# Early scores, a second queue for the moves, and a last product in halves

## The chip, the cores and the metric

One core of a Trainium2 chip runs the whole program. The metric is device time in microseconds. Five engines matter: TensorE (matmuls, in rows of the profile PE, its weight loads PEld), VectorE (DVE), ScalarE (ACT), GpSimd (POOL, nearly unused here) and SyncE (SP), which issues most transfers; a transfer can also be issued by ScalarE, and such rows have the engine name ACTq.

## The reference

`x` is 8 batches x 8 heads x 512 tokens x 64, `state` 8 x 8 x 32 x 64. For each batch and head:

```
a     = softmax(x state^T / 8)  over the 32 states;   xread = a state        (512 x 64)
a2    = softmax(state x^T / 8)  over the 512 tokens;  sread = a2 x           (32 x 64)
rows  = concat(xread, sread), heads side by side: 8 x 544 rows of 512
h     = rows w_in          (512 x 2048)
out   = (h * clip(h + 3, 0, 6) / 6) w_out     (2048 x 512)
```

All in float32, 4352 rows out.

## The kernel before

**Tiling.** `rows w_in` is not formed from `xread`: for the tokens, `state w_in` (called W', `wprime`) is made first and the softmax weights `aT` are multiplied with it. The work is a list of `steps`, each one batch and one block of 128 columns of `w_in`: `first(n)` makes h for 512 tokens in one of two `ps_h` banks, ScalarE and VectorE turn it into g (lines 908 and 910) and split g into two float32r halves (lines 246 and 247), and `second(n)` multiplies them with `w_out` into four accumulators `acc0` to `acc3`, two steps later (`LAG`). Each float32 product is three float32r matmuls (`product`, line 858). The chunk of 4 steps for batch 0 alone, steps 0 to 3, uses plain float32 (lines 887 and 927), because the halves of its weights are not ready then. The steps run: batch 0 chunk 0, batch 1 chunks 0 and 1, batch 0 chunks 1 to 3, batch 1 chunks 2 and 3, then batches 2 to 7, and last the `sread` rows of all batches (b equal to B, 256 rows, 2 accumulators).

**Scores.** For each batch the scores x state^T are wanted twice. `scores_by_columns` puts them with states along the partitions, 16 matmuls into two banks (`all_heads`, line 462); `states(b)` makes the softmax over tokens from them: maximum (714), exponential (718), sums and reciprocals (721, 723). `tokens_by_rows` (batch 0, line 620) and `tokens_by_columns` (batch 1 and later) make the softmax over states, lines 574 to 591, and turn it into `aT` (639 and 644 for batch 0). For batch 1 the scores by columns are copied out of PSUM (line 686) and kept for `states(1)`; for batch 0 they are made a second time, inside `late`, told at step 8 with rank 2.35 and name "L", in the two `ps_s` banks, and `states(0)` reads them there. Line 540 (`put_state`) copies a batch's turned state out of PSUM; line 555 turns x and line 560 copies it.

**Moves.** `weights_moved(1)` turns the exponentials of batch 1 block by block: VectorE transposes 32 x 32 blocks (766), then 32 small transfers of 16 KB (line 773), all issued by SP, place the blocks; `tokens_read(1)` (line 815) reads the result, in one go on TensorE with batch 2's scores.

**Order.** Nothing is scheduled by hand and nothing by the hardware: `Plan` collects operations with an engine (T, V, S, Q for TensorE, VectorE, ScalarE, SP), a cost in us, a rank and the tiles they read and write. `order` then goes through a model of the time: for each engine it takes, among the operations that can start within 0.3 us of the earliest (0.8 for ranks up to 0), the one with the lowest rank; `URGENT` is rank -20. Slots of tiles are limited: `st_raw` has one, `tmp` ten, each accumulator one. What comes out is a fixed order of instructions on every engine; an instruction that has to wait holds up all behind it on its engine. Until the first product TensorE is kept at work with transposes of the identity into a spare bank (line 1157, `idle`). The rank of a step's work is its number n; the weights' ranks stand in the table `weights` (told, kind, block, blocks, place, rank of preparing, rank of loading), prepared on ScalarE and VectorE by lines 308 to 327 and split by 352 and 354.

**The end.** For b equal to B the two accumulators are evicted by VectorE (`acc0`, line 954) and ScalarE (`acc1`, line 951), scaled by 1/6, and stored by SP and by ScalarE (both rows show line 969).

## Time and profile before

| | us |
|---|---|
| median of 3 runs (659.68 to 659.81) | 659.69 |
| the profiled execution | 660.08 |
| its span, first to last instruction | 658.2 |
| TensorE busy (98%) | 647.7 |
| VectorE busy (64%) | 420.4 |
| ScalarE busy (47%) | 312.1 |

The granted TensorE clock is 0.999 of full speed, that is 2.4 GHz throughout. Matmuls are pipelined and their ends modelled: a matmul of 512 columns has a row of 0.39 us, but the next one starts 0.23 us later, so starts are to be compared, not durations. `PE ps_h L887 x4` is four matmuls of line 887 that write a `ps_h` bank. In a timeline row the brackets give the idle time just before the instruction and who ended it. A line can be that of a helper.

### The profile page before, as it was taken

The numbers are of one execution on the slowest core, as the hardware profiler recorded it, in microseconds if no ns is written. First come the engines' busy times: TensorE is split into PE (matmuls) and PEld (weight loads), VectorE is DVE, ScalarE is ACT, GpSimd is POOL, SyncE is SP. The second block draws the span as 40 slices with busy tenths as digits, with TensorE's granted clock in tenths as the row PEclk, the third lists the DMA queues.
The fourth block names the chain that finished last, engine by engine and source line by source line (L and its number), as shares of the span: only waits on it lengthen the run. The fifth ranks groups of instructions, "written<-read, shape, count | busy, mean of one in ns | idle before, by whom it ended". The sixth has DMA issues, their size and how long they took to land.

```text
span 658.2 us, 9905 instructions
## 1 busy us (share of the span) xinstructions
PE 647.7 (98%) x3934; PEld 502.1 (76%) x3934; DVE 420.4 (64%) x697; ACT 312.1 (47%) x522; POOL 1.0 (0%) x7
## 2 busy tenths in 40 slices
PE   7999999999999999999999999999999999999997
PEld 7447777777777877787877877787778788788896
DVE  4999999977756845954577356934595353443552
ACT  5889686643524543533444343534344343333542
POOL 0000000000000000000000000000000000000000
PEclk9999999999999999999999999999999999999999
DMA  8904742415163043323050504041131001000101
GB/s 266 318 1 160 196 150 106 98 27 138 19 144 58 15 75 85 66 32 65 17 116 14 83 1 121 13 64 32 64 66 28 5 1 65 0 1 1 64 1 33
DMA packets 130895, 46.26 MB, mean 70 GB/s; under 512 B 119201, under 2 KB 121249, under 8 KB 130721
## 3 DMA queue, kind: packets, MB, share of 16 engines
q1 hardware_dynamic: 130704, 45.37, 27.9%
q8 instruction: 31, 0.51, 0.3%
q10 hardware_dynamic: 144, 0.26, 0.1%
q14 instruction: 16, 0.12, 0.1%
HBM read 33.03 MB, written 8.91 MB: 64 GB/s over the span
## 4 chain that ended last, share of the span: by engine, by line
PE 89%; SPq 6%; DMA 2%; DVE 1%; issue 1%; ACT 0%; DVEq 0%; ACTq 0%
PE acc L858 51%; PE ps_h L858 27%; PE ps_s L462 4%; SPq L773 2%; PE acc L927 2%; SPq L787 2%; PE ps_h L462 2%; SPq L449 1%; PE ps_h L887 1%; PE ps_h L815 1%; DMA ot<-in_x_dram 1%; DMA tmp<-tmp 1%; PE ps_s L620 1%; DMA st_raw<-in_state_dram 0%; DMA raw<-in_x_dram 0%
## 5 line engine op out<-in xcount | busy, mean ns | idle before, releaser
L858 PE MATMUL acc<-w_out_hi,g_hi 128*128 128x512 f32 x528 | 208.9, 396 | 0.0
L858 PE MATMUL acc<-w_out_lo,g_hi 128*128 128x512 f32 x528 | 205.9, 390 | 0.0
L858 PE MATMUL acc<-w_out_hi,g_lo 128*128 128x512 f32 x528 | 205.7, 390 | 0.1
L908 ACT ACTIVATE g<-ps_h,three 128x512 f32<-128x512 f32 (+1 forms) x144 | 95.7, 664 | 211.3 <-PE ps_h L858 210.4
L910 DVE SCALAR_TENSOR_TENSOR g<-g,ps_h 128x512 f32<-128x512 f32 (+1 forms) x144 | 94.6, 657 | 134.6 <-ACT g L908 133.3
L858 PEld LDWEIGHTS acc<-w_out_hi,g_hi 128*128 128x128 f32 x528 | 99.1, 188 | 34.0 <-issue 11.3
L246 ACT CAST g_hi<-g 128x512 fp32r<-128x512 f32 (+1 forms) x140 | 83.2, 596 | 81.6 <-DVE g L910 81.1
L247 DVE TENSOR_TENSOR g_lo<-g,g_hi 128x512 fp32r<-128x512 f32 (+1 forms) x140 | 92.0, 658 | 46.0 <-ACT g_hi L246 44.2
L858 PEld LDWEIGHTS acc<-w_out_hi,g_lo 128*128 128x128 f32 x528 | 99.1, 188 | 21.5 <-DVE g_lo L247 0.6
L858 PEld LDWEIGHTS acc<-w_out_lo,g_hi 128*128 128x128 f32 x528 | 99.2, 188 | 19.1
L858 PE MATMUL ps_h<-aT_hi,wp_hi 128*128 128x512 f32 (+1 forms) x248 | 90.6, 365 | 0.0
L858 PE MATMUL ps_h<-aT_hi,wp_lo 128*128 128x512 f32 (+1 forms) x248 | 89.8, 362 | 0.0
L858 PE MATMUL ps_h<-aT_lo,wp_hi 128*128 128x512 f32 (+1 forms) x248 | 89.7, 362 | 0.0
L858 PEld LDWEIGHTS ps_h<-aT_hi,wp_hi 128*128 128x128 f32 x248 | 46.8, 189 | 8.5 <-DVE g L910 0.5
L858 PEld LDWEIGHTS ps_h<-aT_lo,wp_hi 128*128 128x128 f32 x248 | 46.8, 189 | 8.2 <-issue 0.5
L858 PEld LDWEIGHTS ps_h<-aT_hi,wp_lo 128*128 128x128 f32 x248 | 46.8, 189 | 7.2
L858 PE MATMUL ps_h<-aT_hi,wp 128*128 128x512 f32 x128 | 44.6, 389 | 0.0
L858 PEld LDWEIGHTS ps_h<-aT_hi,wp 128*128 128x128 f32 x128 | 24.0, 188 | 5.0
L858 PE MATMUL ps_h<-aT_lo,wp 128*128 128x512 f32 x64 | 24.9, 389 | 0.0
L462 PE MATMUL ps_s<-w_in,stT 64*32 64x512 f32 (+1 forms) x368 | 22.9, 555 | 0.0
L546 DVE STREAM_TRANSPOSE tmp<-raw 128x512 f32<-128x512 f32 x24 | 16.4, 698 | 7.1 <-DMA raw<-in_x_dram 7.1
L247 DVE TENSOR_TENSOR wp_lo<-ps_s,wp_hi 128x512 fp32r<-128x512 f32 (+1 forms) x34 | 19.7, 618 | 0.0
(123 smaller groups left out, 504.7 us busy)
## 6 DMA issues: line engine op xcount, KB each, us to landing
out_dram<-ot SPq DMA_DIRECT2D x8, 1024.0 KB, 4.4
early<-in_moe_w_in_dram SPq DMA_DIRECT2D x7, 1024.0 KB, 6.7
xb<-in_x_dram SPq DMA_DIRECT2D x28, 256.0 KB, 4.3
raw<-in_x_dram SPq DMA_DIRECT2D x96, 64.0 KB, 2.1
early<-in_moe_w_out_dram SPq DMA_DIRECT2D x4, 1024.0 KB, 5.8
raw<-in_moe_w_out_dram SPq DMA_DIRECT2D x7, 512.0 KB, 5.3
raw<-raw SPq DMA_DIRECT2D x96, 32.0 KB, 1.9
early<-in_moe_w_in_dram SPq DMA_DIRECT2D x2, 512.0 KB, 5.9
```

The lines of the kernel that those rows point to most:

```text
L246: S_(cost, rank, lambda: nc.scalar.copy(hi(), src()), reads, [writes[0]])
L247: V(cost, rank, lambda: nc.vector.tensor_tensor(lo(), src(), hi().bitcast(F32), op=ALU.subtract), [*reads, writes[0]], [writes[1]])
L449: nc.sync.dma_start(t[rows, i].rearrange("t (a c) -> t a c", c=NS), x[b, 4 * g + 2 * i + u, :, k * NS : (k + 1) * NS].rearrange("(a t) c - ...
L462: nc.tensor.matmul(out[u][cols, :], made["stT", b][rows, cols], moving(q)[rows], start=True, stop=True,)
L546: V(0.7, rank, lambda q=q, key=key: nc.vector.transpose(xT(b, q), made[key][:, q % 2]), [(*key, q % 2, u, k) for u in range(2) for k in ra ...
L620: nc.tensor.matmul(out[:, j, q], xT(b, q)[:, js], apart[:, q], start=True, stop=True,)
L773: nc.sync.dma_start(dst[:, :, q], src[:, :, c])
L787: nc.sync.dma_start(dst[:, :, q], src[:, :, c])
L858: nc.tensor.matmul(ps, l, r, start=start and k == 0, stop=stop and k == n - 1)
L908: S_(cost + 0.05, rank, lambda: nc.scalar.activation(g(), bank(ps)[:, :width], AF.Relu, bias=three), [ps], [g_key])
L910: V(cost, rank, lambda: nc.vector.scalar_tensor_tensor(g(), g(), 6.0, bank(ps)[:, :width], op0=ALU.min, op1=ALU.mult), [ps], [g_key])
L927: nc.tensor.matmul(bank(acc), made["g_hi", n][:, js], plain_out[i][1](), start=opens, stop=closes)
```

## The change

Five things. (1) `scores_by_columns(0)` is called right behind `tokens_by_rows(0)` with rank -1.21 and the banks `acc0` and `acc1`; a new `keep` copies the result to two `tmp` tiles on ScalarE with rank 0.85, and `late` calls `states(0)` on these. (2) In `weights_moved(1)` the 16 moves of g = 1 are issued by ScalarE, with rank 22 + 2.6. (3) The last product, `acc1` of the last step, is made in two halves of 256 columns, evicted by VectorE and ScalarE and stored by SP and ScalarE; `acc0` is evicted by ScalarE instead of VectorE. (4) Many ranks of the start change, the order of loading w_out 0 and w_in 2 among them. (5) `states(1)` moves: its ranks were 10.97 + 5 x 5.31 = 37.5 and are 8.24 + 5 x 0.50 = 10.7.

```diff
--- before.py
+++ after.py
@@ -658,9 +658,15 @@
                   lambda g=g: a_first(g), [("w_in2", "a", g, k) for k in range(2)],
                   [("aT", 0, g, "hi"), ("aT", 0, g, "lo")])
 
-    def scores_by_columns(b, rank, after=(), name="C"):
-
-        ps = [("ps_s", (name, b, u)) for u in range(NG)]
+    def keep(b, rank, ps):
+
+        for g in range(NG):
+            S_(0.6, rank, lambda g=g: nc.scalar.copy(tmp(kept_key(b, g)), bank(ps[g])),
+               [ps[g]], [kept_key(b, g)])
+
+    def scores_by_columns(b, rank, after=(), name="C", banks=None):
+
+        ps = [(banks[u] if banks else "ps_s", (name, b, u)) for u in range(NG)]
         riders = [tokens_read(b - 1, "ps_h")] if b >= TURNED else []
 
         def run():
@@ -681,10 +687,7 @@
 
         hi_lo = weights_of(b)
         if b < TURNED:
-
-            for g in range(NG):
-                S_(0.6, URGENT, lambda g=g: nc.scalar.copy(tmp(kept_key(b, g)), bank(ps[g])),
-                   [ps[g]], [kept_key(b, g)])
+            keep(b, URGENT, ps)
         for g in range(NG):
             bt_key = ("tmp", ("bt", b, g))
             V(0.62, URGENT if b < TURNED else rank(2) - 0.5, lambda g=g, bt_key=bt_key: nc.vector.transpose(
@@ -767,11 +770,14 @@
                     tmp(key), tmp(("tmp", ("e2", b, g)))), [("tmp", ("e2", b, g))], [blocks_key], after)
                 for c in range(P // NS):
                     for q in range(NQ):
-                        def move(c=c, q=q, g=g, key=blocks_key):
+                        def move(c=c, q=q, g=g, key=blocks_key, queue=(nc.sync, nc.scalar)[g]):
                             src = tmp(key)[quarter(q)].rearrange("p (j c n) -> p j c n", j=J, n=NS)
                             dst = e2T(b, g)[quarter(c)].rearrange("p (j q n) -> p j q n", j=J, n=NS)
-                            nc.sync.dma_start(dst[:, :, q], src[:, :, c])
-                        Q(rank, 16.384, move, [blocks_key], [e2T_key(b, g, c, q)])
+                            queue.dma_start(dst[:, :, q], src[:, :, c])
+                        if g:
+                            S_(0.5, rank + 2.6, move, [blocks_key], [e2T_key(b, g, c, q)])
+                        else:
+                            Q(rank, 16.384, move, [blocks_key], [e2T_key(b, g, c, q)])
             return
         blocks_key = ("raw", ("blocks", b))
         made_of = lambda key: get(key, lambda: stage.tile([P, NG, S], F32, name="raw"))
@@ -859,6 +865,7 @@
                 k += 1
 
     first_of = {}
+    HALVES_OF_LAST = [slice(0, DO // 2), slice(DO // 2, DO)]
 
     def first(n):
         b, i, _, _ = steps[n]
@@ -930,6 +937,19 @@
                 hi, lo = made["g_hi", n], made["g_lo", n]
                 w = [w_out_of(h, i, 1)[:, 0, :] for h in ("hi", "lo")]
                 product(bank(acc), [((hi[:, js], lo[:, js]), w)], opens, closes)
+
+            def run_half(cols, closes, js=js, acc=acc):
+                hi, lo = made["g_hi", n], made["g_lo", n]
+                w = [w_out_of(h, i, 1)[:, 0, cols] for h in ("hi", "lo")]
+                product(bank(acc)[:, cols], [((hi[:, js], lo[:, js]), w)], False, closes)
+            if n == len(steps) - 1 and j == nt - 1:
+
+                halves = []
+                for k, cols in enumerate(HALVES_OF_LAST):
+                    halves.append(T(0.37, n + LAG + 0.5, lambda k=k, cols=cols, run_half=run_half: run_half(cols, k == 1),
+                                    [("g_hi", n), ("g_lo", n), w_out_key(i, "hi"), w_out_key(i, "lo"), acc],
+                                    [(*acc, k)], halves))
+                continue
             if plain(b, i // FPC):
                 T(0.9, n + LAG + 0.5, run, [("g_hi", n), (*plain_out[i][0], "lo")], [acc])
             else:
@@ -947,7 +967,13 @@
                 V(0.68, rank, lambda j=j, acc=acc: nc.vector.scalar_tensor_tensor(
                     ot()[:, j, :], bank(acc), 1.0 / 6.0, ot()[:, j, :], op0=ALU.mult, op1=ALU.add),
                     [acc], [(*ot_key, j)])
-            elif (j % 2 == 0 or i < NF - 1) if b < B else j == nt - 1:
+            elif b == B and j == nt - 1:
+                one, two = HALVES_OF_LAST
+                V(0.37, rank, lambda j=j, acc=acc: nc.vector.tensor_scalar_mul(
+                    ot()[:, j, one], bank(acc)[:, one], 1.0 / 6.0), [(*acc, 0)], [(*ot_key, j, 0)])
+                S_(0.34, rank, lambda j=j, acc=acc: nc.scalar.mul(
+                    ot()[:, j, two], bank(acc)[:, two], 1.0 / 6.0), [(*acc, 1)], [(*ot_key, j, 1)])
+            elif b == B or j % 2 == 0 or i < NF - 1:
                 S_(0.62, rank, lambda j=j, acc=acc: nc.scalar.mul(ot()[:, j, :], bank(acc), 1.0 / 6.0),
                    [acc], [(*ot_key, j)])
             else:
@@ -964,14 +990,13 @@
         else:
 
             ov = out.rearrange("(b s) e -> s b e", s=TOK)
-            for j in range(nt):
-                rows = slice(S + j * P // B, S + (j + 1) * P // B)
-                store = lambda queue, j=j, rows=rows: queue.dma_start(ov[rows], ot()[:, j, :])
-                if j < nt - 1:
-                    Q(n, 262.0, lambda store=store: store(nc.sync), [(*ot_key, j)])
-                else:
-
-                    S_(0.6, n, lambda store=store: store(nc.scalar), [(*ot_key, j)])
+            rows = lambda j: slice(S + j * P // B, S + (j + 1) * P // B)
+            for j in range(nt - 1):
+                Q(n, 262.0, lambda j=j: nc.sync.dma_start(ov[rows(j)], ot()[:, j, :]), [(*ot_key, j)])
+            j, (one, two) = nt - 1, HALVES_OF_LAST
+            Q(n, 131.0, lambda: nc.sync.dma_start(ov[rows(j)][..., one], ot()[:, j, one]), [(*ot_key, j, 0)])
+
+            S_(0.6, n, lambda: nc.scalar.dma_start(ov[rows(j)][..., two], ot()[:, j, two]), [(*ot_key, j, 1)])
 
     def w_in_split(c, rank, after):
 
@@ -1011,15 +1036,16 @@
     seen = set()
 
     weights = [
-        (0, "in", 0, 1, ("early0", 0, 0), 16.36, -26.80), (1, "in", 1, 1, ("early0", 0, 1), -6.71, -8.31),
-        (2, "in", 2, 2, ("early1", 0), -1.27, -6.98), (0.63, "out", 0, 1, ("raw", ("out", 0)), 1.26, -6.68),
-        (-7.79, "out", 1, 1, ("raw", ("out", 1)), 0.25, 2.20), (-4.38, "out", 2, 1, ("raw", ("out", 2)), 3.78, -2.50),
-        (5.36, "out", 3, 1, ("early3", 0, 0), 1.98, -3.33),
+        (0, "in", 0, 1, ("early0", 0, 0), -7.43, -30.31), (1, "in", 1, 1, ("early0", 0, 1), -3.56, -8.86),
+        (2, "in", 2, 2, ("early1", 0), 0.77, -7.40), (-0.50, "out", 0, 1, ("raw", ("out", 0)), -1.65, -7.60),
+        (-1.36, "out", 1, 1, ("raw", ("out", 1)), -0.37, -1.69), (2.37, "out", 2, 1, ("raw", ("out", 2)), 3.03, -1.98),
+        (5.32, "out", 3, 1, ("early3", 0, 0), 1.66, -1.44),
     ]
     SOONER = (4.0, 4.0, 5.0, 7.0)
     LATE_TOLD, AGAIN, MOVED = (8, 12), 16.0, 22
     READ_WITH = (12, 0)
-    LATE, LATE_STEP, HALVES = (2.35, 10.97), (0.16, 5.31), 6.21
+    KEPT = (-1.21, 0.85)
+    LATE, LATE_STEP, HALVES = (2.35, 8.24), (0.38, 0.50), 3.35
     PLACES = {
         ("in", 4): ("early0", 1), ("in", 6): ("early1", 1), ("out", 4): ("early2", 1),
         ("out", 6): ("early3", 1), ("in", 8): ("early2", 2), ("in", 10): ("early3", 2),
@@ -1090,13 +1116,13 @@
         at(step + 1, lambda: load_x(b, step + 0.2, [first_of[step]]))
         at(turned + 1, lambda: load_turned(b, turned + 0.1, [first_of[turned]]))
 
-    at(6, lambda: [f(4.13 + 0.2 * k) for k, f in enumerate(late_halves)])
+    at(6, lambda: [f(5.35 + 0.2 * k) for k, f in enumerate(late_halves)])
     at(9, halves_of_first, 9.5)
     for b, s0 in (0, 4), (1, 8):
 
         def late(b=b, s0=s0):
             rank = lambda k: LATE[b] + k * LATE_STEP[b]
-            states(b, rank, None if b else scores_by_columns(b, LATE[b] + 0.01, (), "L"))
+            states(b, rank, None)
             if b == 0:
                 weights_turned(b, rank(7))
             else:
@@ -1118,12 +1144,13 @@
         s = last - 4 if c == 0 else last + 2 * c - 3
         at(max(s + 1, last + 2 * c - 3), lambda c=c, s=s: w_in_split(c, s + 0.4, [first_of[s]]))
 
-    load_x(0, -14.96)
+    load_x(0, -14.37)
     weights_until(0.7)
     load_state(1, -4.23)
     accs = [f"acc{q}" for q in range(NQ)]
-    take_in(0, -14.56, (), accs)
-    tokens_by_rows(0, lambda k: -2.51, lambda k: (), accs)
+    take_in(0, -11.57, (), accs)
+    tokens_by_rows(0, lambda k: -2.69, lambda k: (), accs)
+    keep(0, KEPT[1], scores_by_columns(0, KEPT[0], (), "L", accs[:NG]))
     load_x(1, -3.76)
     for n in range(len(steps)):
         tell(n)
@@ -1138,14 +1165,14 @@
             for f0, f1 in zip(wp_parts[b, c], ends):
                 weights_until(n + f1 - 1)
                 s = n - 3 + f0
-                wprime(b, [(c, f0, f1)], s + 0.40 if n else (9.65, -6.50, 1.00)[f0],
+                wprime(b, [(c, f0, f1)], s + 0.41 if n else (-16.63, -4.10, -0.69)[f0],
                        ["acc2", "acc3"] if n == 0 and f1 < 3 else None,
                        [first_of[s]] if n >= 8 else (),
                        [tokens_read(0, "ps_h")] if (n, f0) == READ_WITH else ())
         if n == 0:
-            take_in(1, -2.13, [scores_at[0]])
-            rank1 = lambda k: (-0.81, 4.10, 1.92, 0.14, 0.41)[k]
-            tokens_by_columns(1, rank1, scores_by_columns(1, 3.10, [wp_at[0, 0, 2]]))
+            take_in(1, -1.83, [scores_at[0]])
+            rank1 = lambda k: (-5.73, -4.80, -1.44, -2.06, 1.20)[k]
+            tokens_by_columns(1, rank1, scores_by_columns(1, 1.99, [wp_at[0, 0, 2]]))
         for f, a in events.get(n, ()):
             f(*a)
         first(n)
```

## Rows read from the trace of the kernel before

**Rows 1.** Stages: busy us (x instructions) of PE, PEld, DVE, ACT, POOL; clock, DMA share, GB/s.
```profile
0.00:24.00 24.00, 18.72 (x166) 16.97 (x167) 13.64 (x29) 13.88 (x27) 0.95 (x7) 1.00 0.90 269
24.00:50.00 26.00, 26.00 (x122) 10.17 (x121) 24.72 (x44) 23.39 (x40) 0.00 (x0) 1.00 0.32 122
50.00:120.00 70.00, 70.00 (x438) 53.47 (x437) 66.83 (x93) 54.47 (x81) 0.00 (x0) 1.00 0.46 144
120.00:150.00 30.00, 30.00 (x155) 22.72 (x154) 24.09 (x42) 14.33 (x26) 0.00 (x0) 1.00 0.38 69
150.00:652.00 502.00, 501.49 (x3055) 397.82 (x3055) 290.40 (x491) 205.44 (x351) 0.00 (x0) 1.00 0.22 48
```

**Rows 2.** Chain of waits of the first 52 us: start us, us, what.
```profile
16.07 3.25 DMA st_raw<-in_state_dram
...
24.20 1.72 PE ps_h L887 x4
...
32.26 1.02 PE ps_s L462 x16
...
49.88 2.29 PE ps_h L858 x10
```

**Rows 3.** Timeline of TensorE, 14 to 25: start us, us, engine, line, operation.
```profile
17.10 1.53 PE L1157 MATMUL ps_h<-ident 128*128 128x128 f32 x12
```

**Rows 4.** Timeline of ScalarE, 14 to 40.
```profile
14.05 1.27 ACT L308 ACTIVATE early<-early,eighth 128x1024 uint32<-128x1024 uint32 x1 [0.69 <-DMA early<-in_moe_w_in_dram]
...
20.56 1.07 ACT L560 COPY w_in<-ps_s 128x512 f32<-128x512 f32 x2 [1.00 <-PE ps_s L555]
22.76 1.25 ACT L644 COPY w_in<-acc 128x256 f32<-128x256 f32 x4 [1.12 <-PE acc L639]
...
39.00 1.07 ACT L686 COPY tmp<-ps_s 128x512 f32<-128x512 f32 x2 [0.38 <-PE ps_s L462]
```

**Rows 5.** Timeline of VectorE, 19 to 50.
```profile
19.79 0.29 DVE L540 COPY stT<-ps_s 128x128 f32<-128x128 f32 x1 [0.61 <-PE ps_s L534]
...
22.53 1.22 DVE L320 SCALAR_TENSOR_TENSOR early<-early 128x1024 uint32<-128x1024 uint32 x1
...
33.37 0.69 DVE L714 TENSOR_REDUCE nm<-ps_s 128x1 f32<-128x512 f32 x1
34.09 0.15 DVE L716 TENSOR_SCALAR nm<-nm 128x1 f32<-128x1 f32 x1
...
37.75 1.23 DVE L320 SCALAR_TENSOR_TENSOR early<-early 128x1024 uint32<-128x1024 uint32 x1
39.62 1.31 DVE L690 STREAM_TRANSPOSE tmp<-ps_s 128x512 f32<-128x512 f32 x2 [0.64 <-ACT tmp L686]
...
48.57 1.29 DVE L247 TENSOR_TENSOR aT_lo<-tmp,aT_hi 128x512 fp32r<-128x512 f32 x2
```

**Rows 6.** The moves (min/median/max ns), step 22 on VectorE and TensorE, and L815.
```profile
L773 SPq DMA_DIRECT2D tmp<-tmp x32: 586/599/988, 129.3 to 150.2; - x32
130.49 0.69 DVE L247 TENSOR_TENSOR g_lo<-g,g_hi 128x512 fp32r<-128x512 f32 x1
136.29 0.39 PE L858 MATMUL acc<-w_out_hi,g_hi 128*128 128x512 f32 x1
152.21 0.61 PE L815 MATMUL ps_h<-xb,tmp 128*32 128x64 f32 x26 [0.37 <-DMA tmp<-tmp]
```

**Rows 7.** The end: timeline, a 128x256 group (busy, mean ns), one stage.
```profile
653.54 0.60 ACT L951 ACTIVATE ot<-acc 128x512 f32<-128x512 f32 x1 [2.68 <-PE acc L858]
653.58 0.61 SPq L969 DMA_DIRECT2D out_dram<-ot  x1
654.17 0.66 ACTq L969 DMA_DIRECT2D out_dram<-ot  x1
L910 DVE SCALAR_TENSOR_TENSOR g<-g,ps_h 128x256 f32<-128x256 f32 x16 | 6.7, 421 | 17.8 <-ACT g L908 17.8
655.00:656.00 1.00, 0.00 (x0) 0.00 (x0) 0.00 (x0) 0.00 (x0) 0.00 (x0) 1.00 0.97 268
```

## Prediction

> **What bounds the kernel now.** I read the stage table first, to learn which engine has idle time in which stage [rows 1]. TensorE has none from 24 to 150 us and 0.51 us from 150 to 652; what else it has lies ahead of 24 us and behind the last matmul. So time is saved in four ways only: work taken off TensorE behind 24 us, a wait removed there, an earlier first product, a shorter tail. VectorE is nearly as full (24.72 of 26 us, then 66.83 of 70), and that is what could give a gain back.
>
> Second, the chain of waits for the start [rows 2]: the first batch's products begin at 24.20, and from there the chain is TensorE. Ahead of them it runs through the second batch's state transfer (3.25 us, landed at 19.32), its transpose and its copy on VectorE, and only then the last steps of the first softmax. Third, TensorE's timeline of that stretch [rows 3]: L1157 are transposes of the identity that fill waiting time, 12 of them in 1.53 us from 17.10. That time is free. Last, the places of the edits: ScalarE and VectorE around the scores, the DMA issues, the tail.
>
> **The change part by part.** The sum is made against the profiled execution: 660.08 us, a span of 658.2 and 1.88 around it. The median of the runs is 659.69, so 0.39 comes off at the end.
>
> *Scores ahead.* `scores_by_columns(0)` leaves its place in the middle of second(0). The chain gives its 16 matmuls 1.02 us there [rows 2], and the product behind them starts a pipeline anew; I take 1.1, between 1.0 and 1.2. Where they go, behind the scores of `tokens_by_rows`, they need `stT` and `xT` of batch 0, which those scores needed too, and 1.1 us fit into the fillers' 1.53 [rows 3]. Cost there: nothing.
>
> What it adds is `keep`: two copies 128x512 on ScalarE, 1.07 us by the same copy for batch 1 [rows 4]. ScalarE waited 1.00 us ahead of batch 1's xT copies and 1.12 us ahead of L644, which hides them. But they must be out of acc0 and acc1 before L639 transposes into these. Between 0 and 1.07 us of the first product's start; 0 taken, the cover being twice the copies. `states(0)` then reads SBUF instead of PSUM with the same instructions, and later by rank (2.35 + 5 x 0.38 = 4.25 against 3.15); off the path.
>
> *New ranks at the start.* The first softmax keeps its neighbours (-2.69 behind w_in 1's -3.56; before, -2.51 behind -6.71). w_out 0 (0.5 MB) is now loaded ahead of w_in 2 and 3 (1 MB). At the 269 GB/s of the first 24 us [rows 1] w_in 2 comes later by 0.524/0.269 = 1.9 us. Its joining on VectorE stood behind the softmax, at 22.53 [rows 5], so the delay meets nobody there, and until it is done TensorE has first(0), first(1) and second(0). Loading fewer bytes first gains nothing by itself. I put the whole at 0, between -0.6 (the copy of the second state, for which VectorE waited 0.61 [rows 5], falls behind the softmax) and +2.4 (below).
>
> The scores of batch 1 move from rank 3.10 to 1.99, ahead of first(2). Their softmax is the longest chain of the start: from L690 at 39.62 to the end of L247 at 49.86, 10.2 us of VectorE, and the product that needs it begins at 49.88 on the chain [rows 2, 5]. There is no slack now, so when TensorE comes 1.1 us sooner this chain must too. It can: between 33.37 and 38.98 VectorE did `states(0)` (two reductions of 0.69, four small steps of 0.15: 2.0 us) and the join of w_in 4 (1.23) [rows 5]. The first serves the read at step 12, the second step 8; the new ranks put both behind the softmax. Given back: 0 to 1.1; I take 0.
>
> *Second batch's transfers.* Now SP issues 32 moves at 0.60 and a gap of 0.04 each, 20.6 us, and L815 stands still for 0.37 us until the last has landed [rows 6]. With 16 on ScalarE's queue SP needs 10.3 us. ScalarE's 16, at 0.60 (SP's) to 0.66 (ScalarE's store [rows 7]), take 9.6 to 10.6 us, in 120 to 150, where it is busy for 14.33 of 30 us [rows 1]. Behind each issue stand L908 and L246 of the next steps. What those may lose is read from step 22: `g_lo` ends at 131.18 and second(22) begins at 136.29, so 5.1 us [rows 6]; seven issues in a row (4.5 us) still pass. The wait goes: -0.4, between -0.6 and +5.5 (below). `states(1)` moves from rank 37 to 11, some 1.7 us of VectorE work brought into 50 to 120, where it has 3.2 us idle [rows 1]: 0 to 1.7, 0 taken because much that it does there is done ahead of need.
>
> *Last products in halves.* TensorE's columns stay the same. The last store now: ScalarE's eviction at 653.54, 0.60; its issue at 654.17, 256 KB; the span ends 4.0 us later [rows 7]. After: acc0's eviction is ScalarE's and its store begins as now. Half one is VectorE's (0.42, a 128x256 step), half two ScalarE's. Read side by side, the last issue is SP's second at 653.58 + 0.61 + 0.04 = 654.2; read in turn, as L690 waited 0.64 for L686's read of the same bank [rows 5], ScalarE's at 653.54 + 0.42 + 0.42 + 0.08 = 654.5. Either way the last issue is no sooner, but has 128 KB, worth 131/268 = 0.5 us if the transfer counts only from its own issue. It does not: the DMA engines are 0.97 busy from 655 to 656 [rows 7], so the 512 KB leave as fast as they can already. I take -0.2, between +0.3 (the later issue) and -0.6; nearest is that full window.
>
> The Trainium skill (DMA: Bandwidth & Descriptors, section "Issuing engines are not separate DMA queues") says that transfers issued by several engines run on the same 16 DMA engines and only the issuing time is saved. By it the cut of the last store gains 0 and the sum is 0.2 smaller; for the moves, whose issuing is the limit, it changes nothing.
>
> **Sum:** -1.1 + 0 + 0 - 0.4 - 0.2 = -1.7. 660.08 - 1.7 = 658.4 for an execution like the profiled one; median 658.0.
>
> **Rivals.**
> *Given back before 55 us.* VectorE being full, the first product of batch 1 stays at 49.9. For: that chain has no slack. Against: 3.2 us of work that can be put off, and scores placed ahead of first(2). The 1.1 is lost: 659.69 - 0.6 = 659.1.
> *First product sooner.* The state's copy falls behind the softmax, -0.6 more: 657.4. For: 0.61 us of pure waiting. Against: transfer, transpose and copy keep their places by rank.
> *Moves without gain.* ScalarE issues them in its gaps alone and ends as late as SP did: 658.4.
> *First product later.* L308 of w_in 2 waited 0.69 for its transfer, with the exponentials behind it on ScalarE [rows 4]. If that order stays, 1.9 us of later transfer and 1.07 of kept copies stand ahead of the softmax, less the 0.6 that VectorE waited anyway: 2.4, net +0.7, 660.4. Against: w_in 2 now has rank 0.77, behind the softmax's -2.69.
> *Slower: the moves in one block on ScalarE.* All 16 have the one rank 24.6, so from step 25 on each of them goes ahead of L908. Sixteen in a row are 10.6 us against 5.1 of slack: TensorE stands 5.5 us, net +4.2, 663.9. It decides from about ten in a row; with twelve, 7.7 - 5.1 = 2.6, net +1.3, 661.0. Against: SP's moves began at 129.3, in step 22 [rows 6], and ScalarE's idle half takes most of the sixteen in the steps before 25.
>
> **How the numbers follow.** Forecast 0.45, its own range 657.5 to 658.5; sooner 0.13; moves without gain 0.08; given back 0.16; later 0.10; block 0.08. The range 656.9 to 659.6 leaves out the block and most of the later start. A measurement here tells 0.2% (1.3 us) from no change, so the line is at 658.37. Faster: most of the forecast, sooner, half of the moves case, 0.55. Same: the given-back case and the rest, 0.32. Slower: the block and the worst of the later start, 0.13.
>
> **What would show it.** L462 on `xT` and `stT` ahead of 22 us and none between the products of second(0); the first product at 24.0, give or take 0.3; the first product of batch 1 near 48.8 with no idle TensorE before it; L773 on two queues with the last landing ahead of L815; no idle TensorE from 140 to 160; the span's end 0.2 us nearer to the last matmul. A first product behind 25.7, or over 0.5 us of idle TensorE between 24 and 150, would make the forecast wrong.

## The result and the profile after

The changed kernel takes 660.68 us (median of 22 runs, 659.38 to 662.3) against 659.57 for the kernel before on the same chip: ratio 1.0016 [1.001, 1.0022]. Forecast was 658.0, range 656.9 to 659.6. So it is 1.1 us slower where 1.7 us less was expected.

The first profiled execution of the changed kernel, "after" below, is one of the two quickest of its 22 (659.38 us, span 657.6); a second profile of the same kernel, "after, again" (660.38 us), stands nearer to the median and is used beside it. Some executions of most kernels have a mean granted clock below 0.998 and are about 1 us longer, and three single ones of 1315 to 3218 us are left out of the medians below.

In the changed kernel the lines have moved: L887 is L894, L908 is L915, L910 is L917, L947 is L967, L815 is L821, L858 is L864, L773 is L776, L690 is L693, and the kept copies of L686 are L664.

The stages of after, with the columns of [rows 1]:

```profile
0.00:24.00 24.00, 19.25 (x179) 16.67 (x180) 13.90 (x30) 15.41 (x30) 0.96 (x7) 1.00 0.92 277
24.00:50.00 26.00, 25.22 (x119) 10.70 (x118) 24.29 (x39) 22.58 (x36) 0.00 (x0) 1.00 0.30 114
50.00:120.00 70.00, 70.00 (x425) 53.39 (x426) 67.42 (x102) 55.80 (x87) 0.00 (x0) 1.00 0.47 145
120.00:150.00 30.00, 29.58 (x151) 22.09 (x150) 22.17 (x36) 12.68 (x22) 0.00 (x0) 1.00 0.45 93
150.00:652.00 502.00, 502.00 (x3060) 398.64 (x3059) 291.03 (x492) 205.74 (x352) 0.00 (x0) 1.00 0.22 46
```

TensorE, without a gap from 24 to 150 us before, now loses 0.78 us in the second stage and 0.42 in the fourth; 0.51 us that were lost behind 150 are gone. Its timeline at the start, where [rows 2, 3] stood:

```profile
15.73 1.06 PE L462 MATMUL acc<-xT,stT 64*32 64x512 f32 x16
16.72 1.20 PE L1184 MATMUL ps_h<-ident 128*128 128x128 f32 x9
...
21.62 1.23 PE L639 MATMUL acc<-ident,tmp 128*128 128x128 f32 x8 [0.42 <-ACT tmp L664]
...
23.56 3.60 PE L894 MATMUL ps_h<-w_in,wp 128*128 128x512 f32 x8
27.09 0.66 PE L462 MATMUL ps_s<-w_in,stT 64*32 64x256 f32 x16
28.27 1.36 PE L462 MATMUL ps_s<-w_in,stT 64*32 64x512 f32 x16 [0.52 <-ACT wp L509]
```

The scores stand ahead of the fillers, at 1.06 us, as forecast, and the first product begins at 23.56 (before, 24.03 in this view). That is no gain of the change: two kernels of the experiments that keep the old start (the tail alone and the moves alone) begin it at 23.50 and 23.40. L639 waits for a kept copy; before, it waited 0.56 at the same place for VectorE's softmax (L591). New is the wait at 28.27, of one group of products of weights and state for the copies of the group before it.

The moves, as groups of issues (min/median/max ns, first and last start) and on ScalarE's timeline:

```profile
L776 SPq DMA_DIRECT2D tmp<-tmp x16: 587/600/784, 128.0 to 138.3; - x16
L776 ACTq DMA_DIRECT2D tmp<-tmp x16: 592/612/890, 129.9 to 143.7; - x16
```

```profile
137.42 0.62 ACT L246 CAST g_hi<-g 128x512 fp32r<-128x512 f32 x1 [0.76 <-DVE g L917]
137.61 6.67 ACTq L776 DMA_DIRECT2D tmp<-tmp  x9
144.38 0.69 ACT L915 ACTIVATE g<-ps_h,three 128x512 f32<-128x512 f32 x1 [6.34 <-DMA tmp<-tmp]
```

Nine of the sixteen stand in a row, 6.67 us, and the next activation comes behind all of them. VectorE and TensorE at that place, after:

```profile
141.89 1.38 DVE L967 SCALAR_TENSOR_TENSOR ot<-acc,ot 128x512 f32<-128x512 f32 x2 [1.32 <-PE acc L864]
145.10 0.69 DVE L917 SCALAR_TENSOR_TENSOR g<-g,ps_h 128x512 f32<-128x512 f32 x1 [1.83 <-ACT g L915]
145.71 0.68 DVE L967 SCALAR_TENSOR_TENSOR ot<-acc,ot 128x512 f32<-128x512 f32 x1
146.48 0.69 DVE L247 TENSOR_TENSOR g_lo<-g,g_hi 128x512 fp32r<-128x512 f32 x1
147.09 0.68 DVE L967 SCALAR_TENSOR_TENSOR ot<-acc,ot 128x512 f32<-128x512 f32 x1
```

```profile
147.83 0.50 PE L864 MATMUL acc<-w_out_hi,g_hi 128*128 128x512 f32 x1 [0.42 <-DVE ot L967]
```

Four accumulators are to be evicted (copied out of their PSUM banks) by L967. Two are; then VectorE stands at the multiplication of g, which needs ScalarE's held activation, and the last two evictions stand behind it, the fourth behind `g_lo` as well. TensorE waits for one of these accumulators. In the kernel before the multiplication stood ahead of the evictions too, but its activation was on time:

```profile
141.35 0.69 DVE L910 SCALAR_TENSOR_TENSOR g<-g,ps_h 128x512 f32<-128x512 f32 x1
142.48 0.69 DVE L947 SCALAR_TENSOR_TENSOR ot<-acc,ot 128x512 f32<-128x512 f32 x1 [0.44 <-PE acc L858]
143.09 0.68 DVE L247 TENSOR_TENSOR g_lo<-g,g_hi 128x512 fp32r<-128x512 f32 x1
143.69 1.88 DVE L947 SCALAR_TENSOR_TENSOR ot<-acc,ot 128x512 f32<-128x512 f32 x3
```

The end of after, beside [rows 7]:

```profile
652.77 0.42 DVE L972 TENSOR_SCALAR ot<-acc 128x256 f32<-128x256 f32 x1 [2.25 <-PE acc L864]
...
653.22 0.38 ACT L974 ACTIVATE ot<-acc 128x256 f32<-128x256 f32 x1 [0.57 <-DVE ot L972]
...
653.64 0.66 ACTq L999 DMA_DIRECT2D out_dram<-ot  x1
```

The last matmul ends at 652.73; VectorE's half begins only then, ScalarE's in turn behind it. The span ends 4.9 us behind that matmul, where it was 4.7.

### The profile page after: what moved, and what is told of

Same layout as the page of the kernel before. It is cut to its first block, busy times and chain, and to the rows that moved or that the text cites. A ratio compares the mean times of both kernels' runs of the same rounds, so it can differ in the third digit from the quotient of the medians.

```text
span 657.6 us, 9909 instructions
## 1 busy us (share of the span) xinstructions
PE 646.8 (98%) x3932; PEld 502.0 (76%) x3932; DVE 419.2 (64%) x697; ACT 313.2 (48%) x525; POOL 1.0 (0%) x7
## 4 chain that ended last, share of the span: by engine, by line
PE 89%; DVE 4%; SPq 4%; ACT 1%; DMA 1%; issue 1%; ACTq 0%
PE acc L864 53%; PE ps_h L864 28%; PE ps_s L462 4%; PE ps_h L462 2%; SPq L776 2%; SPq L417 1%; PE ps_h L821 1%; DMA st_raw<-in_state_dram 1%; DVE g L917 1%; PE ps_h L894 1%; SPq L303 1%; ACTq L776 0%; PE acc L934 0%; SPq L375 0%; DVE g_lo L247 0%
## 5 line engine op out<-in xcount | busy, mean ns | idle before, releaser
L864 PE MATMUL acc<-w_out_hi,g_hi 128*128 128x512 f32 x529 | 209.2, 396 | 0.4 <-DVE ot L967 0.4
L864 PE MATMUL acc<-w_out_lo,g_hi 128*128 128x512 f32 x529 | 206.0, 389 | 0.0
L864 PE MATMUL acc<-w_out_hi,g_lo 128*128 128x512 f32 x529 | 205.7, 389 | 0.0
L915 ACT ACTIVATE g<-ps_h,three 128x512 f32<-128x512 f32 (+1 forms) x144 | 95.7, 665 | 208.9 <-PE ps_h L864 202.2
L917 DVE SCALAR_TENSOR_TENSOR g<-g,ps_h 128x512 f32<-128x512 f32 (+1 forms) x144 | 94.4, 657 | 134.2 <-ACT g L915 133.2
L864 PEld LDWEIGHTS acc<-w_out_hi,g_hi 128*128 128x128 f32 x529 | 99.3, 188 | 34.9 <-issue 13.0
L246 ACT CAST g_hi<-g 128x512 fp32r<-128x512 f32 (+1 forms) x140 | 83.1, 595 | 84.5 <-DVE g L917 84.0
L864 PEld LDWEIGHTS acc<-w_out_hi,g_lo 128*128 128x128 f32 x529 | 99.3, 188 | 21.1
L864 PEld LDWEIGHTS acc<-w_out_lo,g_hi 128*128 128x128 f32 x529 | 99.4, 188 | 19.0
L864 PE MATMUL ps_h<-aT_hi,wp_hi 128*128 128x512 f32 (+1 forms) x248 | 90.5, 365 | 0.0
L864 PE MATMUL ps_h<-aT_hi,wp_lo 128*128 128x512 f32 (+1 forms) x248 | 89.7, 362 | 0.0
L864 PE MATMUL ps_h<-aT_lo,wp_hi 128*128 128x512 f32 (+1 forms) x248 | 89.7, 362 | 0.0
L864 PEld LDWEIGHTS ps_h<-aT_lo,wp_hi 128*128 128x128 f32 x248 | 46.8, 189 | 8.4 <-DVE aT_lo L247 0.3
L864 PEld LDWEIGHTS ps_h<-aT_hi,wp_hi 128*128 128x128 f32 x248 | 46.8, 189 | 8.3 <-ACT aT_hi L246 0.3
L864 PEld LDWEIGHTS ps_h<-aT_hi,wp_lo 128*128 128x128 f32 x248 | 46.8, 189 | 7.2
L864 PE MATMUL ps_h<-aT_hi,wp 128*128 128x512 f32 x128 | 44.6, 389 | 0.0
L864 PEld LDWEIGHTS ps_h<-aT_hi,wp 128*128 128x128 f32 x128 | 24.0, 188 | 5.0
L864 PE MATMUL ps_h<-aT_lo,wp 128*128 128x512 f32 x64 | 24.9, 389 | 0.0
L462 PE MATMUL ps_s<-w_in,stT 64*32 64x512 f32 (+1 forms) x368 | 23.3, 555 | 0.8 <-ACT wp L509 0.5
L546 DVE STREAM_TRANSPOSE tmp<-raw 128x512 f32<-128x512 f32 x24 | 16.3, 697 | 6.6 <-DMA raw<-in_x_dram 6.6
```

Source lines behind the costliest of these rows:

```text
L246: S_(cost, rank, lambda: nc.scalar.copy(hi(), src()), reads, [writes[0]])
L462: nc.tensor.matmul(out[u][cols, :], made["stT", b][rows, cols], moving(q)[rows], start=True, stop=True,)
L546: V(0.7, rank, lambda q=q, key=key: nc.vector.transpose(xT(b, q), made[key][:, q % 2]), [(*key, q % 2, u, k) for u in range(2) for k in ra ...
L864: nc.tensor.matmul(ps, l, r, start=start and k == 0, stop=stop and k == n - 1)
L915: S_(cost + 0.05, rank, lambda: nc.scalar.activation(g(), bank(ps)[:, :width], AF.Relu, bias=three), [ps], [g_key])
L917: V(cost, rank, lambda: nc.vector.scalar_tensor_tensor(g(), g(), 6.0, bank(ps)[:, :width], op0=ALU.min, op1=ALU.mult), [ps], [g_key])
```

## The experiments

Each kernel was timed beside the kernel before on the same chip; ratios are to it. Not all stood on one chip, and differences of 0.1 to 0.3 us between kernels on different chips are not clear of noise. Diffs are against the changed kernel unless said.

**Whose 1.1 us is it?** All moves back on SP, tail and start as changed:

```
-                            queue.dma_start(dst[:, :, q], src[:, :, c])
-                        if g:
-                            S_(0.5, rank + 2.6, move, [blocks_key], [e2T_key(b, g, c, q)])
-                        else:
-                            Q(rank, 16.384, move, [blocks_key], [e2T_key(b, g, c, q)])
+                            nc.sync.dma_start(dst[:, :, q], src[:, :, c])
+                        Q(rank, 16.384, move, [blocks_key], [e2T_key(b, g, c, q)])
```

> The changed kernel, but all 32 moves of the second batch's blocks are issued by SP again (16 more issues of 0.60 us there). Theory A (the block of issues on ScalarE holds the evictions behind it for 6.3 us and longer in most executions, and TensorE then waits near 147 us): the wait near 147 us is gone, the runs lie close together like those of before, and the median is 658.4 to 659.0. Theory B (the new order of the start is sensitive to when the loads land, and loses there in most executions): the median stays at 660.2 to 661.0 and the runs stay apart by 1.5 us or more. Theory D (two stores at the end make the end of the program longer): 660.2 to 661.0 too, but with the runs close together.

659.29 us (11 runs), ratio 0.9995 [0.9987, 1.0004], a little over theory A's range, and no wait of TensorE near 147 us. Theories B and D fall. The changed kernel again, unaltered:

> The changed kernel unaltered, for a second profiled execution. Its time is 660.0 to 661.3 by every theory. If the profile is of a usual execution, theory A wants 1 to 3 us of TensorE waiting between 140 and 152 us, where the first profile has 0.6; theory B wants a first product later than 24.0 us, or 0.5 us or more of further idle time of TensorE before 50 us; theory D wants the last product still near 652.7 us and more than 5 us behind it.

660.9 us (11 runs), ratio 1.0025 [1.0012, 1.0038]; beside the run above, on the same chip, the moves on ScalarE cost 1.6 us. Its trace on ScalarE and TensorE:

```profile
137.53 7.49 ACTq L776 DMA_DIRECT2D tmp<-tmp  x9
145.12 0.69 ACT L915 ACTIVATE g<-ps_h,three 128x512 f32<-128x512 f32 x1 [7.21 <-DMA tmp<-tmp]
```

```profile
147.18 0.50 PE L864 MATMUL acc<-w_out_hi,g_hi 128*128 128x512 f32 x1 [0.67 <-DVE ot L967]
148.56 0.50 PE L864 MATMUL acc<-w_out_hi,g_hi 128*128 128x512 f32 x1 [0.41 <-DVE ot L967]
```

Here the nine issues took 7.49 us instead of 6.67; one of the sixteen took 1297 ns, where the longest of after took 890. TensorE waits 1.08 us instead of 0.42. So, by these two executions, the changed kernel's time varies with how long its row of issues happens to be.

The tail alone on the kernel before (diff against that):

```
+            if n == len(steps) - 1 and j == nt - 1:
...
+                for k, cols in enumerate(HALVES_OF_LAST):
...
+            S_(0.6, n, lambda: nc.scalar.dma_start(ov[rows(j)][..., two], ot()[:, j, two]), [(*ot_key, j, 1)])
```

> The kernel before, with the last product, its two scalings and its store in halves and nothing else of the change. Theories A and B: the time of the kernel before within 0.3 us, 659.3 to 659.9. Theory D: 0.7 to 1.3 us slower than before, 660.3 to 660.9.

659.86 us, 0.11 over its before; ratio 0.9999 [0.999, 1.0007]. Theory D falls again; no gain of the tail shows.

The moves alone on the kernel before (diff against that):

```
-                            nc.sync.dma_start(dst[:, :, q], src[:, :, c])
+                            queue.dma_start(dst[:, :, q], src[:, :, c])
+                        if g:
+                            S_(0.5, rank + 2.6, move, [blocks_key], [e2T_key(b, g, c, q)])
```

> The kernel before, with 16 of the 32 moves issued by ScalarE and nothing else of the change. Theory A: slower than before by 0.5 to 1.5 us, 660.1 to 661.1, with runs 1 us or more apart, and TensorE waiting between 140 and 155 us for an eviction. Theories B and D: 659.2 to 659.6, since the wait of 0.37 us for the last block near 152 us is gone and nothing takes its place.

663.15 us, ratio 1.005 [1.0038, 1.0062]: 3.4 us slower, well over what theory A said. Its trace, on ScalarE and TensorE, and by stages (columns as in [rows 1]):

```profile
139.29 7.19 ACTq L773 DMA_DIRECT2D tmp<-tmp  x9
146.59 0.69 ACT L911 ACTIVATE g<-ps_h,three 128x512 f32<-128x512 f32 x1 [7.34 <-DMA tmp<-tmp]
```

```profile
148.66 0.50 PE L861 MATMUL acc<-w_out_hi,g_hi 128*128 128x512 f32 x1 [2.06 <-DVE ot L950]
```

```profile
146.00:150.00 4.00, 1.56 (x6) 0.66 (x4) 2.60 (x5) 2.86 (x5) 0.00 (x0) 1.00 0.06 9
150.00:153.50 3.50, 3.47 (x8) 2.79 (x9) 2.46 (x4) 0.62 (x1) 0.00 (x0) 0.51 0.73 300
```

The row ends 2.2 us later than in after and 1.5 later than in "after, again", with TensorE within 0.1 us of the same place, and here too two evictions stand behind the waiting multiplication. TensorE stands 2.06 us, and after that its granted clock is 0.51 for 3.5 us (the lower level, 1.2 GHz): its matmuls start 0.43 us apart instead of 0.23, so a wait of 2 us is paid nearly a second time. All five runs have a mean clock of 0.997.

**What of the row holds TensorE?** The same sixteen issues on ScalarE at rising ranks, so that the last nine stand as 3, 1, 4 and 1:

```
-    S_(0.5, rank + 2.6, move, ...)
+    S_(0.5, rank + 2.6 + 0.15 * (NQ * c + q), move, ...)
```

> The changed kernel with its 16 issues on ScalarE at rising ranks, so that the last nine stand as blocks of 3, 1, 4 and 1 with the evictions of g and the casts between them, in place of nine in a row. Theory A1 (it is the row that is too long: an eviction behind it comes 1 to 2 us too late): no wait of TensorE over 0.2 us between 140 and 149 us, 658.7 to 659.4. Theory A2 (it is the sum of the issue time, 16 at 0.65 us on an engine that has no such time to spare there): TensorE still waits, 660.3 to 661.3.

658.58 us, ratio 0.999 [0.9982, 0.9999], no wait near 147 us. A2 falls: ScalarE has the time, the order is at fault. But a longer row did not behave as A1 said. Charging each issue 0.65 puts eleven in a row:

```
-    S_(0.5, rank + 2.6, move, ...)
+    S_(0.65, rank + 2.6, move, ...)
```

> The changed kernel with each issue on ScalarE charged at 0.65 us in place of 0.5 in the order's simulation; the order that comes out has eleven issues in a row in place of nine, and no fewer before them. Theory A1: two more issues at a pitch of 0.65 us are 1.3 us more of waiting for TensorE near 147 us, 661.9 to 662.9, and more where TensorE's granted clock falls after the longer wait. Theory A2: 660.5 to 661.3 as the changed kernel, since the sum on ScalarE is the same.

659.03 us (10 runs), ratio 0.999 [0.9982, 0.9999]: faster than the changed kernel, with a longer row and an activation as late as in "after, again" (145.12). Both theories were wrong. The trace shows why; ScalarE, then VectorE:

```profile
137.22 7.82 ACTq L776 DMA_DIRECT2D tmp<-tmp  x11
145.15 0.69 ACT L915 ACTIVATE g<-ps_h,three 128x512 f32<-128x512 f32 x1 [7.31 <-PE ps_h L864]
```

```profile
141.70 2.76 DVE L967 SCALAR_TENSOR_TENSOR ot<-acc,ot 128x512 f32<-128x512 f32 x4 [1.32 <-PE acc L864]
145.87 0.69 DVE L917 SCALAR_TENSOR_TENSOR g<-g,ps_h 128x512 f32<-128x512 f32 x1 [1.41 <-ACT g L915]
```

The other cost also turned VectorE's order: all four evictions stand ahead of the waiting multiplication, and TensorE is not held there. (It is 0.45 us over the spread issues; its trace loses 0.4 near 195 us, where `g_lo` stands behind a transposition, L546, that waits for x.) TensorE's order changed in two places as well, so this run alone doesn't show the cause. It gave theory V, tested with the row of nine left alone; the line is that of the evictions, L967:

```
-                V(0.68, rank, lambda j=j, acc=acc: nc.vector.scalar_tensor_tensor(
+                V(0.68, rank + -0.6, lambda j=j, acc=acc: nc.vector.scalar_tensor_tensor(
```

> The changed kernel with its nine issues in a row on ScalarE as they are; only VectorE's order is changed near 144 us (and in the same way once more, some 50 us later): the four evictions of the accumulators now stand in a row ahead of the multiplication of g, which waits for ScalarE; in the changed kernel two of them stand behind it. Theory V (TensorE is held by accumulators whose evictions stand behind the waiting multiplication on VectorE): no wait over 0.2 us between 140 and 150 us although ScalarE is held as long as before, 658.5 to 659.2. Theory A1 (the held activation itself reaches TensorE): 660.3 to 661.3, as the changed kernel.

658.54 us (11 runs, 658.44 to 658.7, the tightest of all), ratio 0.9985 [0.9976, 0.9993]; ScalarE, then VectorE:

```profile
137.35 6.01 ACTq L776 DMA_DIRECT2D tmp<-tmp  x9
143.46 0.69 ACT L915 ACTIVATE g<-ps_h,three 128x512 f32<-128x512 f32 x1 [5.50 <-DMA tmp<-tmp]
```

```profile
141.76 2.76 DVE L967 SCALAR_TENSOR_TENSOR ot<-acc,ot 128x512 f32<-128x512 f32 x4 [1.26 <-PE acc L864]
144.44 0.68 DVE L917 SCALAR_TENSOR_TENSOR g<-g,ps_h 128x512 f32<-128x512 f32 x1
```

Theory V holds: one rank on VectorE takes 2.1 us off the changed kernel's 660.68. This profile's row is shorter than any of the changed kernel's, but the eleven's is longer than either and harmless at this place too.

TensorE's matmuls have the same order in this kernel and in the changed one, so their starts can be compared. "After, again" and this kernel both begin the group of L462 in this stretch at 139.74; the next row of L839, in this order:

```profile
150.74 0.27 PE L839 MATMUL ps_h<-ident,tmp 128*128 128x128 f32 x1
149.07 0.27 PE L839 MATMUL ps_h<-ident,tmp 128*128 128x128 f32 x1
```

The 1.67 us between them arise at the two products that wait for accumulators; from 24 us to 146 and from 150 to the last matmul the distance of the two traces changes by no more than 0.1. So the whole difference of these two executions (660.38 and 658.64) lies at this place. (It is more than the 1.08 us in the brackets, which count from the modelled ends of matmuls.) The same comparison gives 0.8 us for after.

**Who else could issue?** The second sixteen on GpSimd:

```
-    queue=(nc.sync, nc.scalar)[g]
+    queue=(nc.sync, nc.gpsimd)[g]
...
-                        if g:
-                            S_(0.5, rank + 2.6, move, [blocks_key], [e2T_key(b, g, c, q)])
-                        else:
+                        if True:
                             Q(rank, 16.384, move, [blocks_key], [e2T_key(b, g, c, q)])
```

> The changed kernel with its second 16 moves issued by GpSimd in place of ScalarE, where nothing stands behind them. If two queues as such help: the wait for the last block near 150 us (0.4 us with all on SP) is gone and nothing takes its place, 658.7 to 659.1. If the second queue gains nothing whatever engine issues: 659.2 to 659.4, as with all on SP. If the issue costs more than 1.3 us each on GpSimd, the last block comes later than from SP: over 659.6.

658.6 us (10 runs), ratio 0.9988 [0.9978, 0.9997], 1.0 under its before; its issues take 551 ns in the median. (The order is made as if SP issued all 32, so ScalarE's is that of the first diff.) Two queues gain what they promise when nothing stands behind them.

**What are the other parts worth?** Start alone: the moves back as in the first diff, and the tail as before.

```
-            if n == len(steps) - 1 and j == nt - 1:
...
-            S_(0.6, n, lambda: nc.scalar.dma_start(ov[rows(j)][..., two], ot()[:, j, two]), [(*ot_key, j, 1)])
+                    S_(0.6, n, lambda store=store: store(nc.scalar), [(*ot_key, j)])
```

> The changed kernel without its moves (all 32 on SP) and without its tail, so that only the new start is left against the kernel before. The kernel with start and tail measured 659.29. Theory: the new start alone gives all of that and the tail nothing, so 659.1 to 659.4, 0.4 to 0.7 us under before, with TensorE's busy time between 24 and 50 us at 25.2 of 26. Rival: the tail costs 0.3 us or more of what the start gives, 658.6 to 658.9.

659.35 us (12 runs), ratio 1.0 [0.9991, 1.001]. The runs lie from 658.32 to 661.97, too far apart to tell the two cases from each other.

The spread issues with the tail taken back in the same way:

> The kernel of the spread issues (658.58) without the tail's halves. If the tail costs 0.2 us or more, as the run of the tail alone (0.1 to 0.2 us over before) and the run of the start alone beside the one of start and tail hint: 657.9 to 658.4. If the tail gains 0.2 us, as forecast: 658.7 to 658.9. If it is nothing: 658.4 to 658.7.

658.44 us against 658.58 with the tail in halves, on another chip; ratio to before 0.9985 [0.9976, 0.9994]. So the tail costs 0.1 if anything: both comparisons say so, and both are within the noise.

The first diff of this section once more:

> Start and tail with all moves on SP once more, beside the same without its moves on SP alone, on one chip. If the second queue gains what its wait near 150 us says (0.4 us) with the gap in other work behind it: 658.9 to 659.3, 0.4 to 0.7 us over the kernels whose second queue holds nobody. If the earlier distance between them was chance: 658.4 to 658.8.

659.0 us, ratio 1.0 [0.9991, 1.0009], and TensorE's wait for the last block is there (`PE ps_h L818 <- DMA tmp<-tmp`, 0.3 us). Beside 658.54 on the same chip (evictions first), the second queue gains 0.46.

The spread issues with the scores in their old place:

```
-    keep(0, KEPT[1], scores_by_columns(0, KEPT[0], (), "L", accs[:NG]))
-            states(b, rank, None)
+            states(b, rank, None if b else scores_by_columns(b, LATE[b] + 0.01, (), "L"))
```

> The kernel of the spread issues (658.58) with the first batch's scores for its states computed after the first products again, as in the kernel before; all other ranks of the start stay. If taking these 8 matmuls (some 1 to 1.1 us) out of TensorE's full stretch is what the start gains: 659.5 to 659.9. If the start's gain comes from the other ranks and loading order: 658.4 to 658.8.

659.8 us, ratio 1.0006 [0.9998, 1.0015]. (It is 16 matmuls that move, not the 8 of the expectation.) Putting the scores back costs 1.2 beside the spread issues and 1.26 beside the evictions first on the same chip.

What the other ranks do, the traces show. From the first product to the group of L462 near 122 us TensorE does the same matmuls in every kernel, but for these 16. First product and group, in the tail alone (old start) and in this kernel, and the group in after (first product at 23.56, above):

```profile
23.50 1.88 PE L888 MATMUL ps_h<-w_in,wp 128*128 128x512 f32 x4
122.35 1.09 PE L462 MATMUL ps_s<-w_in,stT 64*32 64x512 f32 x16
```

```profile
23.71 1.55 PE L894 MATMUL ps_h<-w_in,wp 128*128 128x512 f32 x3 [0.21 <-ACT w_in L644]
123.53 1.09 PE L462 MATMUL ps_s<-w_in,stT 64*32 64x512 f32 x16
```

```profile
122.30 1.09 PE L462 MATMUL ps_s<-w_in,stT 64*32 64x512 f32 x16
```

That is 98.85, 99.82 and 98.74 us. The three traces with the old start agree on 98.85, ten with the new one lie from 98.71 to 98.76 (an eleventh, the base below, has 98.92). So the early scores gain 1.1 us there and the other ranks lose 1.0. Most of the loss is the wait at 28.27: between the two groups that meet there 0.89 us pass from one matmul's start to the next, where these matmuls stand 0.05 us apart on average in the old order.

**What eats part of it?** The last two kernels have VectorE's evictions first and the old tail; the first also separates the two groups of L462 that meet at 28.27:

```
-    (-16.63, -4.10, -0.69)[f0]
+    (-16.63, -4.10, 0.6)[f0]
```

> The kernel of the other run of this call, but the third part of the first chunk's product of weights and state gets the rank 0.60 in place of -0.69: one second product of TensorE stands between it and the part before, which uses the same two PSUM banks. If the start's missing gain of about 0.5 us is the wait of the one for the copies of the other (0.5 us near 28 us): no such wait, and 0.3 to 0.5 us under the other run, 657.9 to 658.2. If that wait is only moved, to the chain of VectorE that ends at the second batch's first product: within 0.2 us of the other run.

> Start and moves as changed, the evictions of the accumulators first on VectorE, and the tail as in the kernel before: by the runs so far (658.54 with the tail in halves, and 0.1 us less without it) 658.3 to 658.6, and no wait of TensorE over 0.2 us from 140 to 150 us.

The base: 658.48, ratio 0.9985 [0.9977, 0.9994], as expected. The other: 661.61, ratio 1.0034 [1.0021, 1.0048], 3.1 us worse. The wait for the copies is gone, but the product that the order now puts there waits longer for its g; and the row on ScalarE came out as ten issues and 8.14 us. TensorE's waits in two stretches, and ScalarE's row:

```profile
PE acc L933 <- DVE g L916: 1.2, 1, 1.2
...
PE ps_h L839 <- DVE g L916: 0.9, 1, 0.9
PE ps_h L864 <- DVE g L916: 0.7, 1, 0.7
```

```profile
139.52 8.14 ACTq L776 DMA_DIRECT2D tmp<-tmp  x10
147.76 0.69 ACT L914 ACTIVATE g<-ps_h,three 128x512 f32<-128x512 f32 x1 [8.69 <-issue]
```

So it settles nothing of the start. It does bound theory V: with the evictions first, an activation at 145.15 is harmless and one at 147.76 costs 1.6 us of waiting. TensorE waits there for the `ps_h` banks that the late multiplication reads, a path that doesn't run through the accumulators.

## Why the prediction was wrong

**Scores ahead, -1.1: right.** They fill the time of the fillers; their place behind 24 us was worth 1.1 (99.82 to 98.74), and putting them back costs 1.2 to 1.26.

**Kept copies, 0: right, within the bound.** L639 waits 0.42 for the first of them, but in two other traces of the new start it waits 0.23 and 0.31 for the softmax instead. The first product is neither sooner nor later by them: 23.38 to 23.56 in ten traces of the new start, against 23.40, 23.50 and 24.03 with the old one, where 24.03 is the execution that the prediction was read from. (Two more traces of the new start have 24.65; in them the granted clock was 0.50, the lower level, for 3.4 us near 10 us.)

**New ranks at the start, 0: this step failed too.** The term measured +1.0 (99.82 against 98.85), inside the bounds named, and ate the gain of the scores: by 122 us the whole start is 0.1 us ahead. The sign that was named for a wrong forecast, over 0.5 us of idle TensorE between 24 and 150, came: 0.78 + 0.42. The rival "given back before 55 us" named this loss but not its way, for the second batch's first product did not stay at 49.9: it begins at 45.69 (before, 49.30 in the same view). What the sum lacked is the wait of one product of weights and state for the copies of the other out of the same two banks, 0.52 us at 28.27, and a wait of 0.26 for w_in's joining at 49.28. Removing the first wait gave no gain, since the one run made for it put a longer one in its place.

**Second batch's transfers, -0.4: this step failed.** Its gain is right: 0.46 when nobody is held. Its cost was put at nothing, because "seven issues in a row (4.5 us) still pass". The row was nine, 6.7 to 7.5 us in the two profiles, and the 5.1 us of slack was the wrong slack twice. For g's own way the slack is larger than that: 7.3 us of holding do no harm if the evictions are first. And it was measured only along L908, L246 and second(), the engine that issues and the data that it makes. What decided stands one engine further: behind the multiplication on VectorE wait two evictions that have nothing to do with the moves. The price is 2.0 to 2.1 us: the changed kernel is 1.11 and 1.15 over its before, and 0.91 under with the evictions first.

The Trainium skill states the rule that was not applied to VectorE here (PSUM — Partial Sum Buffer, section "Engine vs sequencer instructions"): the queues of ScalarE, VectorE and GpSimd are strictly first in, first out. This case agrees: L967 at 145.71 starts behind L917, although the same eviction, the third, starts at 143.08 in the kernel of the eleven, where the waiting multiplication stands behind it.

**The slower rival named the right place and the wrong path.** "The moves in one block on ScalarE" had 0.08; its point was ten in a row, its price for twelve +1.3, and its path the time that second() waits for g. At nine the changed kernel is 1.1 slower, by the evictions.

**Tail, -0.2: no gain, within its bounds.** Both halves are evicted in turn and behind the last matmul; 0.1 is lost, if anything.

**Sum as measured,** each beside its own before: start and tail -0.45, the second queue -0.46, its row of issues +2.0, together +1.1, which is the result. These are differences of the same few kernels, so they close by construction. Start and tail are not clear of no change (0.9995 [0.9987, 1.0004] and 1.0 [0.9991, 1.0009]); the traces give the start 0.1 us up to 122, and where the rest of the 0.45 would arise is open.

## What to carry to other kernels

An engine that issued a DMA was blocked for 0.6 us each time here. Before a row of issues goes on a computing engine, write down the first instruction behind it, who waits for that, and everything that stands behind the waiter on the waiter's own in-order engine: an eviction with no part in the change may be there. Put the evictions of accumulators ahead of an instruction that can be held (2.1 us here); and if an idle engine can issue, as GpSimd here, no one is held.

## What was not expected of the hardware

- The time of one move's issue is steady but for single outliers: 0.60 and 0.61 us in the median on SP and ScalarE in most traces, 0.55 on GpSimd, with the longest of a trace between 0.75 and 1.64 us on SP and ScalarE. The same row of nine took 5.8 to 7.5 us.
- In the run of the moves alone, a stretch in which TensorE stood 2.06 and 0.41 us was followed by 3.5 us at a granted clock of 0.51; a stretch with waits of 0.67 and 0.41 us, in "after, again", was not (its clock stays 1.00 to the end of the last product).
